# State rows ahead of the second stage, block sums on VectorE, two xo buffers, last rows stored in parts

## The chip, the core and the metric

The kernel runs on one core of a Trainium2 chip. The metric is the device time of one execution in microseconds. A core has TensorE (PE: matmuls, with PEld for the weight loads), VectorE (DVE), ScalarE (ACT), GpSimd (POOL) and SyncE (SP, which here issues all DMAs). Each engine runs its own instructions in order and waits on semaphores for the others.

## The reference

Three steps, all in fp32:

```
x: (8, 8, 512, 64), state: (8, 8, 32, 64)          # batch, head, row, dim
a  = softmax(x @ state^T / 8);  xread = a @ state   # per batch and head
a2 = softmax(state @ x^T / 8);  sread = a2 @ x
X  = concat(xread, sread) per batch -> (8 * 544, 512)
h  = X @ w_in (512 x 1024); s = h * softmax(h)
ln = (s - mean) / sqrt(var + 1e-6) * g;  X2 = ln @ w_out (1024 x 512)
out = leaky(X2 @ w_in2 (512 x 2048)) @ w_out2 (2048 x 512)     # leaky(v) = max(0.01 v, v)
```

The weights come as 64-bit floats and are narrowed in the kernel. Each batch has 512 x rows and 32 state rows; the 8 x 32 state rows are gathered into one block of 256 rows, which the code calls batch 8 (`B`).

## The kernel before, in words

Every matrix is kept as a high and a low part (`hi`, `lo`), and each product is three matmuls (`mm3`, L98 to L103): hi times hi, hi times lo, lo times hi. A split is a cast on ACT and a subtraction on DVE (L105 to L107) or on POOL.

*First stage.* For each batch: attention, then h (`h1`, L391) for four blocks of 128 rows, softmax and layer norm on those rows (`solu_norm`, L363), transposes (`tr`, L419), and the second product by w_out (`x2`, L439) in four parts. Each part is copied by ACT into the buffer xo (L453) and stored by SP to a scratch tensor xs in DRAM (L454). For the state rows `h1s` (L405) forms the first product in four steps from srs, the split of the collected state rows (`split_srs`, L799), with w_in loaded again in four parts (`load_wi`, L183); its norm follows in the last step, and `x2` for batch 8 has two parts.

*Second stage* (`second`, L748). Batches go in four pairs, hidden columns in eight chunks of 256. For each pair and chunk, `h2` (L642) forms the four blocks of the hidden layer with seven block products in place of eight (sums and differences of blocks of the weights, S1 to S4, and of x, T1 to T4), accumulating in PSUM banks X, Z and Y, and `out2` (L674) multiplies by w_out2 and adds into oacc on DVE (L689), eight tiles per chunk, through four PSUM banks. For the first pair the chunk's weights are prepared as well: `split_chunk` (L516) narrows them on DVE (L152 to L159), forms the block sums on POOL (L528 to L532), splits them and stores them to scratch, from where later pairs load them. The state rows go through the second stage during the first pair: `h8` (L708) and `out8` (L725), whose x is loaded from xs by `load_x8` (L695) and split by `split_x8` (L700). In the kernel before `h8` and `out8` of a chunk run in the next chunk's iteration, and the second product of the state rows runs between the two halves of chunk 0. `first_x2` (L565) loads and splits x for the first pair, `load_x2`, `diff_x2` and `swap_x2` (L587 to L604) for the others; at a pair's last chunk `out2` stores each batch's 512 rows in one DMA (L692).

*The order.* The list PROGRAM (L839) emits the first stage: a letter names a function (dictionary `emit`, L805) and the digits its arguments; E is the second stage. The order of emission is a priority: the tile framework's planner orders each engine's instructions by it and by its own estimate of when each can start, allots buffers with the same tag (`bufs` of them) and sets all waits. Instructions of different steps can thus be interleaved on an engine; on the chip each engine keeps the planned order.

Of the kernel before, what the change touches and what calls it, by code (L numbers as in the profile page):

```python
# [20 lines left out]
P = 128  # L21
# [17 lines left out]
def attn_solu_leaky_kernel(  # L39
# [399 lines left out]
    def x2(b, u):  # L439
# [4 lines left out]
        for j in range(nd):  # L444
            d = slice((nd * u + j) * P, (nd * u + j + 1) * P)
            for f in range(NF):
# [4 lines left out]
                )  # L451
        o = slot("xo", [P, nd, nt], F32, f"xo{b}_{u}", bufs=1)
        nc.scalar.copy(o, pt.rearrange("p (j t) -> p j t", j=nd))  # L453
# [62 lines left out]
    def split_chunk(c, kind):  # L516
# [3 lines left out]
        if kind == 0:  # L520
# [6 lines left out]
            a11, a12, a21, a22 = v[:, 0, 0], v[:, 1, 0], v[:, 0, 1], v[:, 1, 1]  # L527
            tt = nc.gpsimd.tensor_tensor  # L528
            tt(s_[0], a21, a22, ALU.add)
# [35 lines left out]
    def first_x2(u):  # L565
# [5 lines left out]
        elif u == 1:  # L571
            tsub("T1", C[:, 1, 0], xin["B12"], xin["B11"])
            tsub("T3", C[:, 0, 1], xin["B22"], xin["B12"])
            split_x2("B11", xin["B11"])
            split_x2("T1", td["T1"])
            split_x2("T3", td["T3"])
        elif u == 2:
            tsub("T2", C[:, 1, 1], xin["B22"], td["T1"])
            tsub("T4", C[:, 0, 0], xin["B21"], td["T2"])
            split_x2("B21", xin["B21"])  # L580
            split_x2("B22", xin["B22"])
        else:
            split_x2("T2", td["T2"])
            split_x2("T4", td["T4"])
# [21 lines left out]
    def split_x2(n, src):  # L606
        t = xb(n)
        split(t[:, 0], t[:, 1], src)
# [32 lines left out]

    def h2(p, c, part, between=None):  # L642
        C = late("C")[:, c % 2]
# [5 lines left out]
        if part == 0:  # L649
            prod(X, p, c, "A11", "B11", True)  # L650
            nc.scalar.copy(C[:, 0, 0], X)  # L651
            prod(Z, p, c, "A12", "B21", True)
            tt(C[:, 0, 0], C[:, 0, 0], Z, ALU.add)  # L653
            prod(X, p, c, "S2", "T2", False)
            nc.scalar.copy(C[:, 1, 0], X)
            prod(Y, p, c, "S1", "T1", True)
            if between is not None:
                h8(between)
            prod(X, p, c, "S3", "T3", False)
# [14 lines left out]
    def out2(p, c, j, rs=(0, 1, 2, 3)):  # L674
# [3 lines left out]
        for r in rs:  # L678
# [9 lines left out]
            else:  # L688
                nc.vector.tensor_tensor(o[:, r, :], o[:, r, :], pt, ALU.add)  # L689
        if c == NC - 1 and rs[-1] == NR - 1:  # L690
            rows = out.rearrange("(b t) d -> b t d", t=ROWS)
            nc.sync.dma_start(rows[2 * p + j, :S, :].rearrange("(p r) d -> p r d", r=NR), o)  # L692

# [54 lines left out]
    def second():  # L748
# [4 lines left out]
        for i, (p, c) in enumerate(seq):  # L753
# [7 lines left out]
            if turn:  # L761
                load_x2(p + 1)
            if not i:
                h2(p, c, 0)
                x2(B, 0)
                h2(p, c, 1)
                x2(B, 1)
                load_x8()
                split_x8()
                split_chunk(1, 1)  # L770
                out2(p, c, 0)
                out2(p, c, 1)
                continue
            h2(p, c, 0, prev[1] if prev[0] == 0 else None)
            if turn:
                diff_x2(p + 1)
                swap_x2("B11", "B21")
            if i > 1:
                out2(*prev, 0)
# [3 lines left out]
            if turn:  # L783
                swap_x2("T1", "T3")
            if i > 1:
                out2(*prev, 1)
            if turn:
                swap_x2("T4", "B22")
            if prev[0] == 0:
                out8(prev[1])  # L790
            if new and new[0] == 0:
# [7 lines left out]
    def split_srs():  # L799
        t = slot("q6", [P, 2, NHP, B * NS], F32R, "srs")  # L800
        split(t[:, 0], t[:, 1], srT)
        return t[:, 0], t[:, 1]
# [49 lines left out]
    S7.1 X5.1 t6.0 h6.2 U7.0 h6.1 A7.0 X5.2 w4.1 X5.3 h6.3 t6.1 A7.1 U7.1 B7.0 B7.1 X5.0 h7.0  # L852
    t6.3 R7 D0 t6.2 X6.2 h7.1 X6.1 h7.2 t7.1 X6.3 t7.0 h7.3 c0.0 c0.1 s X6.0 D1 t7.2 w4.0 w4.2 G0 d0.0 G1 G2
    t7.3 D2 w4.3 G3 d0.1 X7.1 X7.0 D3 X7.3 t8.0 X7.2 t8.1 E
"""
# [30 lines left out]
```

## Time and profile before

| | |
|---|---|
| timed runs | 1225.47, 1223.44, 1223.0 us; median 1223.44 us |
| profiled execution | 1218.0 us |
| its span in the trace | 1216.2 us |
| TensorE busy | 1149.7 us (95%), 5416 matmuls |
| VectorE / ScalarE / GpSimd busy | 809.2 (67%) / 496.3 (41%) / 367.6 us (30%) |
| chain that ended last | PE 71%, DVE 12%, POOL 5%, issue 4%, ACT 4%, DMA 3% |
| granted clock, mean | 0.985 |

All times in the rows are from the start of the span. The profiled execution is shorter than the timed ones; sums are made against it. The page gives busy shares of the whole span, which has stages with different limits; the tables by stretch show one stage at a time.

### The profile page before, as it was taken

Reading aid. Unit: us, or ns where it says so; the run is one execution under the profiler, and the core shown is the slowest. Engines: PE = TensorE matmul, PEld = TensorE weight load, DVE = VectorE, ACT = ScalarE, POOL = GpSimd, SP = SyncE. Lnnn points to the kernel's source line nnn. Section 1 sums busy time; section 2 is a strip of 40 time slices with the busy share of each in tenths; the row PEclk is TensorE's granted clock in tenths of the full one; section 3 lists DMA queues with packets and bytes.
Section 4 is the critical chain, followed back from the end, with each engine's and each line's share of the span. In section 5 each row is a group of like instructions: output and inputs, shape, how many; then the busy total and the mean of one; then the engine's idle time right before and its main releaser. Section 6 shows DMA issues by size and latency. Waiting matters only on the chain.

```text
span 1216.2 us, 14127 instructions
## 1 busy us (share of the span) xinstructions
PE 1149.7 (95%) x5416; PEld 949.5 (78%) x5416; DVE 809.2 (67%) x1224; ACT 496.3 (41%) x783; POOL 367.6 (30%) x246
## 2 busy tenths in 40 slices
PE   4768999999999998989999999999999999999998
PEld 2647888878888887877777788888888888888886
DVE  6998777886787587568886872545864547634544
ACT  3565656565565445444333423222432224232221
POOL 2432202202112024566655421323222222223231
PEclk9879999999999999989999999999999999999999
DMA  9432332152062155454554375444564343635331
GB/s 305 166 94 37 120 107 55 63 148 70 24 185 78 44 190 207 180 202 176 209 212 153 150 259 207 158 153 149 203 241 169 134 178 125 255 120 193 112 131 70
DMA packets 65868, 183.38 MB, mean 151 GB/s; under 512 B 39560, under 2 KB 39560, under 8 KB 53512
## 3 DMA queue, kind: packets, MB, share of 16 engines
q1 hardware_dynamic: 65800, 182.47, 42.6%
q8 instruction: 43, 0.70, 0.2%
q14 instruction: 25, 0.20, 0.1%
HBM read 135.27 MB, written 47.19 MB: 150 GB/s over the span
## 4 chain that ended last, share of the span: by engine, by line
PE 71%; DVE 12%; POOL 5%; issue 4%; ACT 4%; DMA 3%; SPq 1%; POOLq 0%; ACTq 0%; DVEq 0%
PE o L101 8%; PE o L102 8%; PE o L103 8%; PE x L101 4%; PE x L103 4%; PE x L102 4%; PE hX L101 4%; PE hX L102 4%; PE hX L103 4%; PE h L101 2%; PE h L103 2%; PE h L102 2%; PE hY L103 2%; PE hY L101 2%; PE hY L102 2%
## 5 line engine op out<-in xcount | busy, mean ns | idle before, releaser
L689 DVE TENSOR_TENSOR oacc<-oacc,o 128x512 f32<-128x512 f32 x224 | 150.4, 684 | 66.1 <-PE o L103 66.0
L101 PE MATMUL x<-ln,w_out_hi 128*128 128x512 f32 (+1 forms) x288 | 110.6, 384 | 3.9 <-ACT xo L453 3.0
L103 PE MATMUL x<-ln,w_out_lo 128*128 128x512 f32 (+1 forms) x288 | 109.8, 381 | 0.0
L102 PE MATMUL x<-ln,w_out_hi 128*128 128x512 f32 (+1 forms) x288 | 109.3, 380 | 0.0
L667 POOL TENSOR_TENSOR gb<-C,gb 128x1024 fp32r<-128x1024 f32 x16 | 47.4, 2964 | 197.7 <-ACT gb L666 182.6
L667 POOL TENSOR_TENSOR gc<-C,gc 128x1024 fp32r<-128x1024 f32 x16 | 46.5, 2905 | 197.1 <-ACT gc L666 197.1
L101 PE MATMUL o<-misc,gc 128*128 128x512 f32 x256 | 99.8, 390 | 1.7 <-DVE oacc L689 1.7
L102 PE MATMUL o<-wo,gb 128*128 128x512 f32 x256 | 99.7, 390 | 0.0
L102 PE MATMUL o<-misc,gc 128*128 128x512 f32 x256 | 99.7, 390 | 0.0
L101 PE MATMUL o<-wo,gb 128*128 128x512 f32 x256 | 99.7, 390 | 0.0
L103 PE MATMUL o<-wo,gb 128*128 128x512 f32 x256 | 99.6, 389 | 0.0
L103 PE MATMUL o<-misc,gc 128*128 128x512 f32 x256 | 99.6, 389 | 0.0
L611 DVE SCALAR_TENSOR_TENSOR C<-C 128x512 f32<-128x512 f32 x64 | 78.0, 1219 | 1.5
L101 PE MATMUL hX<-xbT,w 128*128 128x512 f32 x192 | 75.9, 396 | 3.0 <-ACT C L651 3.0
L614 ACT ACTIVATE C<-hX 128x512 f32<-128x512 f32 x32 | 19.1, 598 | 142.8 <-PE hX L103 142.8
L102 PE MATMUL hX<-xbT,w 128*128 128x512 f32 x192 | 75.6, 394 | 0.0
L103 PE MATMUL hX<-xbT,w 128*128 128x512 f32 x192 | 75.6, 394 | 0.0
L101 PEld LDWEIGHTS x<-ln,w_out_hi 128*128 128x128 f32 x288 | 54.6, 190 | 15.0 <-ACT xo L453 3.3
L661 DVE TENSOR_TENSOR C<-C,hY 128x512 f32<-128x512 f32 x32 | 21.9, 685 | 65.2 <-ACT C L660 65.1
L653 DVE TENSOR_TENSOR C<-C,hZ 128x512 f32<-128x512 f32 x32 | 22.0, 686 | 64.6 <-PE hZ L103 63.1
L101 PE MATMUL h<-sw,a1T 128*128 128x512 f32 x128 | 54.9, 431 | 8.5 <-DVE e(0, 0)_491 L370 4.1
L102 PEld LDWEIGHTS x<-ln,w_out_hi 128*128 128x128 f32 x288 | 54.7, 190 | 10.3 <-DVE r L259 0.2
(736 smaller groups left out, 2956.0 us busy)
## 6 DMA issues: line engine op xcount, KB each, us to landing
w<-w2s SPq DMA_DIRECT2D x24, 2048.0 KB, 7.8
wi<-wsc SPq DMA_DIRECT2D x16, 1024.0 KB, 6.4
w2s<-w SPq DMA_DIRECT2D x8, 2048.0 KB, 7.6
wo<-wo2s SPq DMA_DIRECT2D x12, 1024.0 KB, 7.3
misc<-wo2s SPq DMA_DIRECT2D x12, 1024.0 KB, 6.2
xs<-xo SPq DMA_DIRECT2D x34, 256.0 KB, 2.4
xn<-in_x SPq DMA_DIRECT2D x32, 256.0 KB, 4.6
raw<-in_moe_w_in SPq DMA_DIRECT2D x8, 1024.0 KB, 5.3
```

The lines of the kernel that those rows point to most:

```text
L101: nc.tensor.matmul(o, ah, bh, start=start, stop=False, **kw)
L102: nc.tensor.matmul(o, ah, bl, start=False, stop=False, **kw)
L103: nc.tensor.matmul(o, al, bh, start=False, stop=stop, **kw)
L611: nc.vector.scalar_tensor_tensor(o, v, 0.01, v, ALU.mult, ALU.max)
L614: nc.scalar.activation(o, v, AF.Copy, scale=0.01)
L653: tt(C[:, 0, 0], C[:, 0, 0], Z, ALU.add)
L661: tt(C[:, 1, 1], C[:, 1, 1], Y, ALU.add)
L667: nc.gpsimd.tensor_tensor(g[:, 1, 0], C[:, 0], f32(g[:, 0, 0]), ALU.subtract)
L689: nc.vector.tensor_tensor(o[:, r, :], o[:, r, :], pt, ALU.add)
```

## The change

Six edits. The buffer xo gets a second copy. The four block sums of a chunk go from POOL to DVE. In `second`, the two parts of `x2` for the state rows, their load and their split come ahead of chunk 0; chunk 0's `out2` goes into chunk 1 as for all other chunks; `h8` of a chunk runs in that chunk (chunk 1 makes 0 and 1), behind the fourth product; `out8` of the chunk before runs behind the second product (in chunk 1 behind the last). The last chunk's rows are stored as each tile of 128 rows is done. srs moves from buffer q6 to q2, and the split of T1, which lies in q2, to the last step of `first_x2`. The end of PROGRAM is reordered: the state rows' first product ahead of chunk 0's weights and of the x splits; `w4.1`, already emitted two lines above, is emitted again.

```diff
-        o = slot("xo", [P, nd, nt], F32, f"xo{b}_{u}", bufs=1)
+        o = slot("xo", [P, nd, nt], F32, f"xo{b}_{u}", bufs=2)
@@ split_chunk
-            tt = nc.gpsimd.tensor_tensor
+            tt = nc.vector.tensor_tensor
@@ first_x2
             split_x2("B11", xin["B11"])
-            split_x2("T1", td["T1"])
             split_x2("T3", td["T3"])
...
         else:
+            split_x2("T1", td["T1"])
             split_x2("T2", td["T2"])
@@ h2
-    def h2(p, c, part, between=None):
+    def h2(p, c, part, first=(), then=()):
...
             tt(C[:, 0, 0], C[:, 0, 0], Z, ALU.add)
+            for f, v in first:
+                f(v)
             prod(X, p, c, "S2", "T2", False)
             nc.scalar.copy(C[:, 1, 0], X)
             prod(Y, p, c, "S1", "T1", True)
-            if between is not None:
-                h8(between)
+            for f, v in then:
+                f(v)
             prod(X, p, c, "S3", "T3", False)
@@ out2
-        if c == NC - 1 and rs[-1] == NR - 1:
-            rows = out.rearrange("(b t) d -> b t d", t=ROWS)
-            nc.sync.dma_start(rows[2 * p + j, :S, :].rearrange("(p r) d -> p r d", r=NR), o)
+            if c == NC - 1:
+                rows = out.rearrange("(b t) d -> b t d", t=ROWS)[2 * p + j, :S, :]
+                nc.sync.dma_start(rows.rearrange("(p r) d -> p r d", r=NR)[:, r], o[:, r, :])
@@ second
+            old = c - 1 if p == 0 else NC - 1 if (p, c) == (1, 0) else -1
+            first = [(out8, old)] if old >= 0 else []
+            then = [(h8, k) for k in ([0, 1] if c == 1 else [c])] if p == 0 and c else []
+            if (p, c) == (0, 1):
+                first = []
             if not i:
-                h2(p, c, 0)
                 x2(B, 0)
-                h2(p, c, 1)
                 x2(B, 1)
                 load_x8()
                 split_x8()
-                split_chunk(1, 1)
-                out2(p, c, 0)
-                out2(p, c, 1)
-                continue
-            h2(p, c, 0, prev[1] if prev[0] == 0 else None)
+            h2(p, c, 0, first, then)
...
-            if i > 1:
+            if i:
                 out2(*prev, 0)
...
             h2(p, c, 1)
...
+            if (p, c) == (0, 1):
+                out8(0)
-            if i > 1:
+            if i:
                 out2(*prev, 1)
...
-            if prev[0] == 0:
-                out8(prev[1])
@@ split_srs
-        t = slot("q6", [P, 2, NHP, B * NS], F32R, "srs")
+        t = slot("q2", [P, 2, NHP, B * NS], F32R, "srs")
@@ PROGRAM
-    t6.3 R7 D0 t6.2 X6.2 h7.1 X6.1 h7.2 t7.1 X6.3 t7.0 h7.3 c0.0 c0.1 s X6.0 D1 t7.2 w4.0 w4.2 G0 d0.0 G1 G2
-    t7.3 D2 w4.3 G3 d0.1 X7.1 X7.0 D3 X7.3 t8.0 X7.2 t8.1 E
+    t6.3 R7 s w4.0 w4.1 D0 t6.2 X6.2 h7.1 X6.1 h7.2 t7.1 X6.3 t7.0 h7.3 G0 G1 w4.2 w4.3 c0.0 c0.1 t7.2
+    X6.0 G2 G3 D1 t7.3 D2 d0.0 X7.1 t8.0 X7.0 t8.1 d0.1 X7.3 D3 X7.2 E
```

## Rows read from the trace of the kernel before

**Rows 1.** Busy time by stretch: start:end, length, then PE, PEld, DVE, ACT, POOL, PEclk, DMA

```profile
430.00:480.00 50.00, 45.38 (x207) 36.87 (x206) 39.20 (x53) 25.61 (x37) 17.93 (x13) 0.97 0.55 200
480.00:560.00 80.00, 74.21 (x379) 62.98 (x377) 55.60 (x54) 35.34 (x48) 49.57 (x28) 0.96 0.57 211
560.00:705.00 145.00, 136.25 (x648) 112.50 (x647) 115.15 (x129) 56.61 (x69) 83.81 (x45) 1.00 0.43 165
618.12:645.64 27.52, 26.36 (x127) 21.91 (x126) 22.47 (x26) 10.72 (x13) 17.89 (x11) 1.00 0.38 153
```

**Rows 2.** TensorE's waits, 430 to 705 us: total us, times, longest us

```profile
PE o L101 <- DVE oacc L689: 9.0, 8, 1.7
PE x L101 <- ACT xo L453: 3.0, 1, 3.0
PE hX L101 <- ACT C L651: 3.0, 1, 3.0
PE hZ L103 <- POOL w L523: 1.7, 1, 1.7
PE x L101 <- ACT ln L106: 0.8, 1, 0.8
PE tr L432 <- DVE e(8, 0)_3976 L388: 0.8, 1, 0.8
```

**Rows 3.** Timeline, 449 to 463 us: start, length, engine, line, operation, idle before

```profile
449.61 3.86 POOL L529 TENSOR_TENSOR ws<-wn 128x256 f32<-128x256 f32 x1 [12.67 <-DVE wn L159]
...
456.69 1.06 ACT L533 CAST w<-ws 128x1024 fp32r<-128x1024 f32 x1 [6.14 <-POOL ws L532]
...
458.60 1.11 ACT L368 ACTIVATE e(8, 0)_3976<-hs,nm(8, 0)_3974 128x1024 f32<-128x1024 f32 x1
...
462.40 0.32 SPq L535 DMA_DIRECT2D w2s<-w  x1
462.81 0.38 SPq L454 DMA_DIRECT2D xs<-xo  x1
```

**Rows 4.** Timeline, 469 to 473 us, around the wait for xo

```profile
469.77 0.59 ACT L453 COPY xo<-x 128x512 f32<-128x512 f32 x1 [1.98 <-DMA xs<-xo]
...
470.41 0.50 PE L101 MATMUL x<-ln,w_out_hi 128*128 128x512 f32 x1 [3.05 <-ACT xo L453]
...
472.31 0.63 PE L103 MATMUL x<-ln,w_out_lo 128*128 128x512 f32 x1
```

**Rows 5.** Timeline, 502 to 520 us: x of the state rows goes out and back

```profile
502.38 0.34 SPq L454 DMA_DIRECT2D xs<-xo  x1
...
506.22 0.37 SPq L696 DMA_DIRECT2D misc<-xs  x1
...
517.15 0.39 PE L102 MATMUL h<-misc,w 128*128 128x256 f32 x1 [0.73 <-DVE misc L703]
```

**Rows 6.** Timeline, 640 to 644 us: the leaky step beside POOL's subtraction

```profile
640.02 2.40 POOL L667 TENSOR_TENSOR gc<-C,gc 128x1024 fp32r<-128x1024 f32 x1 [5.24 <-ACT gc L666]
...
641.11 2.38 DVE L611 SCALAR_TENSOR_TENSOR C<-C 128x1024 f32<-128x1024 f32 x1
```

**Rows 7.** POOL's groups, 430 to 720 us: busy us, mean ns, idle before

```profile
L529 POOL TENSOR_TENSOR ws<-wn 128x256 f32<-128x256 f32 x8 | 13.7, 1715 | 20.6 <-DVE wn L159 20.6
...
L531 POOL TENSOR_TENSOR ws<-wn 128x256 f32<-128x256 f32 x8 | 6.3, 792 | 0.0
```

**Rows 8.** DVE's groups, 430 to 720 us: busy us, mean ns, idle before

```profile
L653 DVE TENSOR_TENSOR C<-C,hZ 128x512 f32<-128x512 f32 x9 | 6.2, 685 | 10.0 <-PE hZ L103 8.5 <-ACT C L651 1.4
...
L563 DVE TENSOR_TENSOR C<-xbB,C 128x1024 f32<-128x1024 f32 x2 | 2.4, 1221 | 0.0
```

**Rows 9.** DVE's timeline, 612 to 690 us: the first difference for the next pair

```profile
666.26 1.23 DVE L563 TENSOR_TENSOR T<-xin 128x1024 f32<-128x1024 f32 x1 [5.08 <-DMA xin<-xs]
```

**Rows 10.** DMA issues: operation, count, KB each, median us from issue to landing

```profile
xs<-xo SPq DMA_DIRECT2D x34, 256.0 KB, 2.4
```

**Rows 11.** Line 882, the end of the program: count, ns min/median/max, first and last start

```profile
L882 SPq EVENT_SEMAPHORE  x7: 17/28/3371, 1211.8 to 1216.2; - x7
```

## The prediction

> **What bounds the kernel now.** I read four views, in this order. First the page: TensorE is busy 95% of the span and leads the chain of waits with 71%, so the time is TensorE's matmuls, which this change does not touch in number, plus the stretches where TensorE stands idle or runs at a lower clock. So the question is only which idle TensorE time goes and which comes.
>
> Second, the table of busy time by stretch [rows 1]. Before 430 us nearly all idle time lies in the first 120 us, ahead of everything in the change. From 430 to 480 us TensorE is idle 50.0 - 45.4 = 4.6 us, from 480 to 560 us 80.0 - 74.2 = 5.8 us, from 560 to 705 us 145.0 - 136.3 = 8.7 us. From 705 us on the page's slices show it full up to the last stores. All that this change can give back therefore lies between 430 and 705 us, where the state rows pass from the first stage to the second and the first pair of batches runs through its eight chunks, and at the end.
>
> Third, the waits of TensorE from 430 to 705 us [rows 2]: 9.0 us in eight waits of the output products for VectorE (DVE) to add an earlier one, 3.0 us for the copy to xo, 3.0 us for the copy of X to C, 1.7 us for a weight low part from GpSimd (POOL), 0.8 us twice for the last row blocks of the first stage, and 0.7 us for the state rows' x [rows 5].
>
> Fourth, the timeline around each. *State rows.* POOL takes its block sums at 449.6 us; the first lasts 3.86 us. ScalarE (ACT) stands with the cast of the sums (L533) until 456.69 us, having waited 6.14 us, and behind it in ACT's order is the exp of the state rows, at 458.60 us [rows 3]. *xo.* SyncE (SP) issues the w2s store of the same chunk at 462.40 us, once POOL is done, and the store of xo, queued behind it, at 462.81 us [rows 3]; the single xo buffer is free again at 469.77 us, and TensorE goes on at 470.41 us after 3.05 us; a matmul then takes 0.63 us [rows 4] instead of the 0.38 us of the page's groups: the clock has fallen from its upper level (2.4 GHz) to the lower (1.2 GHz) for a while after the idle time, and the stretch has a granted clock of 0.97, the next one 0.96, against 1.00 from 560 us on [rows 1]. *x of the state rows.* Its last part is stored at 502.38 us, SP issues the load at 506.22 us, and the product can start at 517.15 us, 0.73 us late [rows 5].
>
> **The change part by part.**
>
> *1. Two xo buffers, and the sums off POOL, 430 to 480 us.* The copy no longer waits for the store in front of it; the sums no longer hold the cast, so the exp of the state rows comes about 5 us earlier, and in the new emission order the state rows' products and norms come ahead of the x splits and chunk 0. Of the 4.6 us I take 3.05 (xo) and 0.8 (e(8,0)) as gone; the 0.8 for the transposes of batch 7 stays, since its norm is not touched. With the xo wait goes the slow clock: 24 matmuls from 470.41 us took some 7.2 us to issue against 24 x 0.227 = 5.4 us at the pace that the output products keep (six in 1.36 us), 1.8 us. Together 5.6 us. Bounds: 0, if something else (the splits on DVE) is as late, and 6.4 us.
>
> *2. The second product of the state rows in front of chunk 0.* It moves 11.5 us of TensorE work (two times 48 half-width matmuls) forward; nothing is added. It frees the w_out buffers earlier, so the weights of chunk 1 are split sooner, and it covers the x splits. Its SP work moves too: two stores of xo and the load of x. Cost: chunk 1 now makes both h8(0) and h8(1), and out2 of chunk 0 is moved into chunk 1, so between the last x2 product and h8(0) only 7 + 4 products of 1.36 us remain, 15.0 us. In the kernel before the read-back of x took 17.2 us: some 2.4 us from the end of the product to the store at 502.38 us, and 14.8 us from there to 517.15 us [rows 5]. That adds a wait of 2.2 us; queued behind it on TensorE is everything. If SP is free sooner than at 506.22 us it vanishes, if the w2s store stands in front of it again it may be 4 us with a slow clock. I take 2.2 us and keep 0 to 4.
>
> *3. Order in the chunk.* h8(c) reads chunk c's weights in chunk c itself instead of in the next one, so the buffer for the chunk after next is free half an iteration sooner; the wait for POOL (1.7 us) goes with it. Two output products of the state rows leave the end of the iteration, where they were the ninth and tenth to ask for one of four banks, and come after two products of 1.36 us. In rows: the leaky of 128x1024 (L611) takes 2.38 us instead of 1.22 us because POOL runs L667 from 640.02 to 642.42 us [rows 6, 8], the adds behind it come late, and the tenth fill waits 1.2 us. With 2.7 us of products in between, a lag of 1.2 us is covered. From 480 to 560 us I take the 5.8 us of idle as gone, and 2.8 us of slow clock behind the 3.0 us wait (27 matmuls from 536.5 to 543.2 us took 6.7 us, at the usual pace 3.9 us); less the 2.2 us of step 2 and 0.8 us for a ragged start, 5.6 us. From 560 to 705 us four such waits of 1.2 us and one of 0.5 us, 5.3 us, go. The other two of 1.7 us each at 668 and 673 us have another cause: DVE stood 5.08 us at the first difference for the next pair, whose x had not landed [rows 9]. The loads still follow the last raw weights; I take one of the two as gone, 1.7 us.
>
> *4. Block sums on DVE.* Four of 128x256 for each of eight chunks. No such row on DVE exists; 128x1024 takes 1.22 and 128x512 0.69 us [rows 8], so 1.04 ns an element and 0.16 us fixed, 0.42 us each, 1.7 us a chunk (lower bound 1.3 us, when the fixed part overlaps; upper bound that one of the four is also held by POOL as L611 was, 1.2 us more). POOL loses the same sums, 1.7 us for the first of them and about 0.8 us for the second [rows 7]. Per iteration DVE has 22.5 of 27.5 us busy, TensorE 26.4 [rows 1]: with 1.7 more, 24.2 us, it stays under TensorE's 26.4 us, but its casual slack falls from 3.9 to 2.2 us. I charge 2.0 us in all (bounds 0 and what the rivals say).
>
> The Trainium skill's page "SBUF — State Buffer" (section "Who interferes with whom") speaks against this part: a DVE instruction with two SBUF inputs and a GpSimd instruction that reads SBUF exclude each other for a whole instruction. The trace agrees: L611, with two SBUF inputs, ends 1.07 us after L667, its own length after POOL's end. By that rule a sum can be held for all of POOL's 2.40 us, so the sum above would lose up to 2.4 us a chunk on DVE; this is the second rival.
>
> *5. Last rows stored in parts.* At the end SP waits 3.37 us for the last 1 MB store [rows 11]. A 256 KB store lands 2.4 us after issue [rows 10], of which 0.34 us is the issue [rows 5]: a wait of 2.05 us, 1.3 us less (bounds 0 and 3.4). The other three parts go out under the products. For earlier pairs six more issues on SP hide under TensorE.
>
> *6. Order of the program, srs in another buffer, one more load of w4.1.* srs no longer waits for the last h, but its product still needs that h's bank; T1 now waits for srs, hidden by the state rows' second product. The extra 1 MB load goes out in a stretch in which the page's DMA row shows one or two tenths. Zero, with 2 us to either side, as the planner orders all of it anew.
>
> **Sum.** 5.6 + 5.6 + 5.3 + 1.7 - 2.0 + 1.3 = 17.5 us. The profiled execution took 1218.0 us (1216.2 us of span): 1200.5 us. The three timed runs have a median of 1223.44 us, 5.4 us above the profiled one; the same gain gives 1205.9 us, and 1206 is my figure.
>
> **The rivals.**
>
> *A. New waits take half of it.* x of the state rows late by 4 us with a slow clock, and a wait of about 1 us in each of five iterations because DVE has little slack. For it: rows 1 and 9, DVE busy and in order. Against: the banks' waits had one cause, and ten fills in a row are gone. Gain 17.5 - 9.5 = 8 us: 1215.5 us.
>
> *B. DVE becomes the bound: slower.* The place is chunks 1 to 6. The sums cost 1.7 us and are held for 2.4 us: 22.5 + 4.1 = 26.6 us busy, and DVE's own waits, 5.0 us an iteration now, have to shrink to zero to stay near TensorE's 26.4 us. If three of them stay, an iteration takes 29.6 us, 2.1 us more than now; six of these are 12.6 us, and the 5.3 and 1.7 us of step 3 do not come; steps 1, 3 (first part) and 5 give back 5.6 + 2.8 + 1.3 us at most. Time 1223.4 + 12.6 - 9.7 = 1226.3 us. It decides from 29.1 us an iteration on. Against it: POOL loses its sums, so the casts for which DVE waits come earlier.
>
> *C. The change does not arrive.* The order of instructions is a planner's, by its own times; it may put the state rows and the sums where they stood, with other waits of the same size. Only xo and the tail remain, less the 2 us of the sums: 3.05 - 2 + 1.3 = 2.3 us, within 0.2%: 1221.1 us.
>
> *D. All waits go,* the clock stays up and DVE keeps pace: 4.6 + 1.8 + 5.8 + 2.8 + 8.7 + 1.3 = 25 us: 1198.5 us.
>
> **How the numbers follow.** Forecast 0.55 (its own range 1200 to 1212 us), A 0.22, B 0.10, C 0.06, D 0.07. About 2.4 us (0.2%) is what a measurement of this kernel can tell from no change. Faster: forecast, A and D, 0.84; same: C, 0.06; slower: B, 0.10. The range runs from D's end to beyond A, 1199 to 1219 us; it leaves out B, C and the last of D.
>
> **What would show it.** Right: no wait of TensorE for xo; the exp of row block (8,0) within 2 us of its maximum; no block sums on POOL and DVE sums of about 0.4 us; iterations of the first pair at 26.4 to 27 us instead of 27.5; at most 2 to 3 us of wait at the first h8; a last wait of SP near 2 us. Wrong: waits of TensorE for oacc of 1 us or more in each chunk, sums on DVE of 1 us or more, or TensorE idle between the last x product of batch 7 and chunk 0.

## The result, and the profile after

The changed kernel is slower: 1234.88 us (median of four runs, 1232.46 to 1235.31) against 1223.22 us for the kernel before beside it, a ratio of 1.0102 [1.0076, 1.0128]. The forecast was 1206 us; the sign is wrong too. With four runs of each kernel the ratio may lean towards one of the two courses that a run can take before the change begins, of which the next paragraph tells.

The profiled execution took 1235.08 us, its span 1232.9 us, 16.7 us more than before. Some 6 us of that are not the change's. TensorE's first 1952 matmuls stand in the same order in both kernels. The 1789th begins R7 (the attention product `sr` of batch 7), yet it starts at 398.58 us in the one and at 404.51 us in the other. Across all profiles it starts either at 397.7 to 399.7 us or at 402.6 to 405.3 us, for kernels with and without the change, so I compare profiles from that product on: 817.6 us before, 828.4 us after, 10.8 us more. The ratio says 12.5 us (0.0102 x 1223).

Where the 10.8 us lie, with the start of a chunk taken at its first product `hX<-xbB` (matmuls that the change moves from one stretch to another are taken out: 11.5 us for the state rows' second product and 2.9 us for one h8): from R7 to chunk 0 +0.4 us; chunks 0 to 2 +1.9; chunks 3 to 7, 139.8 us before and 145.7 us now, +5.8; the rest, with a tail 1.5 us shorter, +2.7.

The table by stretch of the kernel after (columns as in [rows 1]; the fourth row is one iteration, the last two are 4 us each, behind a wait of TensorE):

```profile
430.00:480.00 50.00, 46.31 (x209) 37.39 (x209) 37.79 (x57) 24.75 (x37) 10.54 (x10) 0.93 0.36 127
480.00:560.00 80.00, 71.39 (x374) 60.45 (x373) 65.59 (x62) 36.14 (x50) 36.13 (x16) 0.96 0.67 247
560.00:705.00 145.00, 134.77 (x629) 111.33 (x627) 115.93 (x137) 50.83 (x63) 67.77 (x28) 0.98 0.46 172
605.09:633.85 28.76, 26.62 (x128) 21.87 (x126) 24.75 (x30) 10.53 (x13) 13.43 (x7) 1.00 0.48 183
456.00:460.00 4.00, 3.02 (x7) 2.22 (x8) 4.00 (x9) 2.74 (x4) 0.28 (x1) 0.56 0.00 0
594.00:598.00 4.00, 2.79 (x9) 2.28 (x10) 2.83 (x6) 1.70 (x3) 1.29 (x1) 0.81 0.58 218
```

Idle TensorE time is 3.7, 8.6 and 10.2 us in the three stretches; it was 4.6, 5.8 and 8.7 us. POOL is far less busy (10.5 instead of 17.9 us in the first, 67.8 instead of 83.8 us in the third), as meant, and TensorE gained nothing from it. The lower clock level was to go with the waits; it came back behind the new ones (0.56 and 0.81 in the last two rows). An estimate of its price: the share of the clock that was not granted, times the length, makes 3.5 + 3.2 + 2.9 = 9.6 us in the three stretches, against 1.5 + 3.2 + 0 = 4.7 us in [rows 1].

TensorE's waits of the kernel after from 430 to 705 us (columns as in [rows 2]):

```profile
PE hX L101 <- ACT C L662: 6.0, 3, 2.0
PE hY L101 <- DVE C L663: 4.5, 2, 2.4
PE h L102 <- DVE misc L705: 3.1, 1, 3.1
PE o L101 <- ACT oacc L742: 2.6, 1, 2.6
PE hX L101 <- ACT C L651: 2.0, 2, 1.3
PE x L101 <- ACT ln L106: 1.8, 1, 1.8
PE x L102 <- DVE ln L107: 1.0, 1, 1.0
PE tr L432 <- DVE e(8, 1)_3955 L388: 0.8, 1, 0.8
PE hX L101 <- DVE C L615: 0.5, 1, 0.5
```

Set beside [rows 2], nearly every name is new. The waits for xo (3.0 us) and for POOL's weight part (1.7 us) are gone, and so are the eight for oacc on L689 (9.0 us). In their place stand three of 2.0 us for the copy of X into C (L662), two for the sum of Y into C (L663), one of 3.1 us for x of the state rows (L705), one for the first tile of the state rows' oacc (L742), and two for the last norm of batch 7 (L106, L107). The total is 22.3 us, where [rows 2] and the 0.7 us for the state rows' x [rows 5] make 19.0 us. So the waits grew by 3.3 us and the clock took about 4.9 us more; together that is the 8.1 us from R7 to the end of chunk 7.

The costliest group, the waits for L662, is shown once in its place. Timeline of the kernel after, the iteration of 605 to 634 us (columns as in [rows 3], the bracket being the engine's idle time ahead of the instruction and what ended it):

```profile
602.38 3.41 POOL L523 TENSOR_TENSOR w<-wn,w 128x1024 fp32r<-128x1024 f32 x1
605.73 2.42 POOL L534 TENSOR_TENSOR w<-ws,w 128x1024 fp32r<-128x1024 f32 x1
605.82 1.15 ACT L151 ACTIVATE wn<-raw 128x1024 f32<-128x1024 f32 x1 [1.22 <-POOL w L523]
608.10 2.87 POOL L674 TENSOR_TENSOR gc<-C,gc 128x1024 fp32r<-128x1024 f32 x1
608.19 1.17 ACT L151 ACTIVATE wn<-raw 128x1024 f32<-128x1024 f32 x1 [1.22 <-POOL w L534]
610.93 2.84 POOL L539 TENSOR_TENSOR wo<-wn,wo 128x1024 fp32r<-128x1024 f32 x1
...
611.44 2.88 DVE L152 TENSOR_SCALAR wn<-wn 128x1024 f32<-128x1024 f32 x1
616.75 0.60 ACT L614 ACTIVATE c<-h 128x512 f32<-128x512 f32 x1 [3.64 <-PE h L103]
...
622.21 0.42 DVE L529 TENSOR_TENSOR ws<-wn 128x256 f32<-128x256 f32 x1
623.34 0.43 DVE L532 TENSOR_TENSOR ws<-wn,ws 128x256 f32<-128x256 f32 x1
623.69 0.68 DVE L615 TENSOR_TENSOR c<-h,c 128x512 f32<-128x512 f32 x1
624.40 0.62 ACT L724 CAST g<-c 128x512 fp32r<-128x512 f32 x1 [7.05 <-DVE c L615]
624.93 0.58 ACT L662 COPY C<-hX 128x512 f32<-128x512 f32 x1
625.56 0.50 PE L101 MATMUL hX<-xbT,w 128*128 128x512 f32 x1 [2.00 <-ACT C L662]
```

Read it from below. TensorE waits 2.00 us for X's bank, which L662 empties. ACT could have done that copy earlier, but the cast L724 stands ahead of it in ACT's order, and that cast waits 7.05 us for the leaky step of h8 on DVE (L615), whose input lay ready at 617.35 us (616.75 + 0.60). DVE comes to it 6.3 us later, because two whole narrowings (their first steps, L151, lie 2.4 us apart; before, two such steps lay 6.7 us apart in one iteration) and the four block sums stand in front, and because POOL works without a break from 600.0 to 613.8 us: L152 takes 2.88 us beside it, against 0.68 to 0.70 us wherever it runs without POOL, in all kernels here. Three engines' orders, none of them full, make one wait.

### The profile page after: what moved, and what is told of

Same layout as the page of the kernel before. It is cut to its first block, busy times and chain, and to the rows that moved or that the text cites. A ratio compares the mean times of both kernels' runs of the same rounds, so it can differ in the third digit from the quotient of the medians.

```text
span 1232.9 us, 14169 instructions
## 1 busy us (share of the span) xinstructions
PE 1158.6 (94%) x5416; PEld 955.0 (77%) x5416; DVE 835.4 (68%) x1256; ACT 494.4 (40%) x783; POOL 335.2 (27%) x214
## 4 chain that ended last, share of the span: by engine, by line
PE 69%; DVE 16%; issue 5%; ACT 4%; POOL 3%; DMA 2%; SPq 1%; POOLq 0%; DVEq 0%; ACTq 0%
PE o L101 7%; PE o L102 7%; PE o L103 7%; PE x L102 5%; PE x L101 5%; PE x L103 5%; PE hX L101 3%; PE hX L102 3%; PE hX L103 3%; PE h L101 2%; PE h L102 2%; PE h L103 2%; PE sr L305 2%; PE tr L432 2%; PE hY L101 2%
## 5 line engine op out<-in xcount | busy, mean ns | idle before, releaser
L611 DVE SCALAR_TENSOR_TENSOR C<-C 128x512 f32<-128x512 f32 x64 | 78.6, 1228 | 1.7
L663 DVE TENSOR_TENSOR C<-C,hY 128x512 f32<-128x512 f32 x32 | 21.9, 686 | 71.8 <-ACT C L662 71.7
L101 PEld LDWEIGHTS x<-ln,w_out_hi 128*128 128x128 f32 x288 | 54.9, 190 | 12.5 <-ACT ln L106 2.4
L102 PEld LDWEIGHTS x<-ln,w_out_hi 128*128 128x128 f32 x288 | 54.9, 191 | 11.5 <-DVE ln L107 1.3
L103 PEld LDWEIGHTS x<-ln,w_out_lo 128*128 128x128 f32 x288 | 54.9, 191 | 10.3
```

The costliest lines, as they stand in the source:

```text
L101: nc.tensor.matmul(o, ah, bh, start=start, stop=False, **kw)
L102: nc.tensor.matmul(o, ah, bl, start=False, stop=False, **kw)
L103: nc.tensor.matmul(o, al, bh, start=False, stop=stop, **kw)
L611: nc.vector.scalar_tensor_tensor(o, v, 0.01, v, ALU.mult, ALU.max)
L663: tt(C[:, 1, 1], C[:, 1, 1], Y, ALU.add)
```

## The experiments

Times are medians; ratios are to the kernel before, run beside each, in brackets the 95% interval. "In us" is a difference of ratios times 1223 us; the two intervals together leave it open by some 3 to 4.5 us. The traces give a second measure, one execution each, from R7 to the end: 817.6 us before and 828.4 us changed; e1 827.2, e2 819.3, e3 834.3, e4 820.6, e5 816.1, e6 830.7, e7 818.4, e8 815.7, e9 816.1, e10 830.3, e11 822.6, e12 816.3, e13 811.3, e14 806.7, e15 822.8, e16 817.1 and e17 816.7 us. Three questions in turn: which part of the change costs, what is behind the part that costs most, and what had caused the waits of the kernel before.

### Which part: one of them undone

**e1: the block sums back on POOL.**

```diff
-            tt = nc.vector.tensor_tensor
+            tt = nc.gpsimd.tensor_tensor
```

> The changed kernel (1234.9 us) with the four block sums of a chunk back on POOL, all else as changed. Theory Q (the order in the chunk: the two narrowings now run back to back on DVE ahead of the state rows' leaky step, the cast of g8 waits for that step at the head of ACT's queue, and the copy of X that frees a PSUM bank waits behind it): the sums are 1.5 us of the 8 us or so that stand in front of the leaky step, so the three waits of 2.0 us get shorter but the other idle time stays; 1228 to 1232 us. Theory S (the sums on DVE are the cost): back to 1223 us or less.

1230.4 us, 1.0075 [1.0052, 1.0097], 3.3 us back, which the noise does not tell from nothing; from R7 on the trace is 1.3 us shorter. The waits for L662 shrink from 2.0 to 0.3 us and chunks 3 to 5 take 27.7, 28.2 and 28.2 us (31.0, 28.8 and 29.9 us in the kernel after): with 1.7 us less ahead of L615, DVE's backlog clears that much sooner. Chunks 0 to 2 give half of that back (2.4 us longer, with waits of 3.3 us for L651 and for L705). So the sums have a part in the waits for L662; that they cost the kernel time is not shown, and the larger part of the loss remains.

**e2: the old loop of the second stage**, all else changed.

```diff
...
-            h2(p, c, 0, first, then)
...
+            h2(p, c, 0, prev[1] if prev[0] == 0 else None)
...
-            if (p, c) == (0, 1):
-                out8(0)
...
```

> The changed kernel with the second stage's loop as before (state rows' second product inside chunk 0, h8 and out8 one chunk later, out2 of chunk 0 in chunk 0); sums on DVE, two xo buffers, stores in parts and the new order of the first stage stay. Theory Q: the iterations of the first pair return from 29.1 us (mean of five) to about 28, the first three chunks lose their waits of 8.6 us; 1220 to 1225 us. Theory S: 1233 to 1236 us.

1225.66 us, 1.0022 [1.0004, 1.004]: the loop alone costs 9.8 us. The iterations are back at 27.54 us with the old wait of 1.18 us for oacc. What remains sits in the first stage; TensorE's waits there, kernel of e2, 430 to 705 us:

```profile
PE tr L432 <- DVE e(8, 1)_3955 L388: 2.2, 1, 2.2
PE x L101 <- ACT ln L106: 1.8, 1, 1.8
...
PE x L102 <- DVE ln L107: 0.9, 1, 0.9
...
PE tr L432 <- DVE e(8, 0)_3930 L388: 0.4, 1, 0.4
```

5.3 us in front of chunk 0. In the kernel after a low clock followed the same waits: 23 matmuls of the part of `x2` that waited took 8.2 us, where 24 take 5.7 us otherwise; in the trace of e2 the granted clock there is 1.00. The new order has used up the state rows' first products before the norm of batch 7's last block is ready; in the old one 24 of them lie behind that block's transposes and cover all but 0.8 us.

**e3: the old first-stage order**, with the new loop (PROGRAM, srs in q6, T1's split as before).

> The changed kernel with the end of the first stage ordered as before (PROGRAM's last lines, srs in q6, T1 split in the second step); loop, sums, xo and stores as changed. Theory Q: the first stage has no part in the loss, 1232 to 1237 us. Theory P (the new order of the state rows' first product costs: waits of 1.8, 1.0 and 0.8 us and a low clock at 455 to 475 us): 1225 to 1229 us.

1238.7 us, 1.0137 [1.0113, 1.0161]: 4.3 us worse still, at the edge of the noise, and 5.9 us by the traces. So the new loop needs the new first stage: in e3 the state rows' second product, ahead of chunk 0, stands 2.78 us for their norm (L107). The two parts don't add.

### The parts of the loop

**e4: h8 behind the fifth product and its copy**, so that L662 comes ahead of the cast.

```diff
             prod(Y, p, c, "S1", "T1", True)
-            for f, v in then:
-                f(v)
             prod(X, p, c, "S3", "T3", False)
             nc.scalar.copy(C[:, 1, 1], X)
             tt(C[:, 1, 1], C[:, 1, 1], Y, ALU.add)
+            for f, v in then:
+                f(v)
```

> The changed kernel with h8 emitted behind the product S3 T3 and its copy instead of in front of it, so that on ACT the copy of X (L660 here) stands ahead of the cast of g8; all instructions are the same. Theory Q: the waits of the hX products for the copy (6.0 us in three) and the low clock behind them go, iterations of 27 to 28 us, 1224 to 1229 us. Theories S and P: 1233 to 1236 us, since DVE's work and the first stage are untouched.

1227.02 us, 1.0031 [1.001, 1.0051], 8.7 us back (7.8 us by the traces). Iterations take 27.1 to 28.5 us. Its waits of TensorE, 430 to 705 us, begin with:

```profile
PE hX L101 <- ACT C L651: 6.1, 4, 2.1
PE o L101 <- ACT oacc L742: 3.1, 1, 3.1
```

L662 is no longer among them. But the narrowings still lie side by side, and their two first steps and a cast of theirs stand right ahead of the next chunk's first copy on ACT (L651): up to 2.1 us.

**e10 and e11: the state rows' second product back between the halves of chunk 0**, alone and with e4's edit.

```diff
+                h2(p, c, 0)
                 x2(B, 0)
+                h2(p, c, 1)
                 x2(B, 1)
                 load_x8()
                 split_x8()
+                split_chunk(1, 1)
+                continue
```

> The changed kernel with the state rows' second product between the two halves of chunk 0 again, all else as changed. If moving it forward is the main cost in the changed kernel too (alone it cost 11 us, e6 against e5): 1223 to 1226 us. If the changed first stage, with the norms ahead of the x splits, has paid for most of it: the stretch from the product R7 to chunk 3 gets 1 to 4 us shorter, 1231 to 1234 us.

> e4 (h8 behind the copy of X) and e10 together, on the changed kernel. Theory Q with both costs additive: 8 us from e4 and what e10 gives, 1219 to 1226 us, ratio to before 0.998 to 1.003. If both work on the same waits: no better than e4, 1.003.

e10 1231.53 us, 1.0076 [1.0053, 1.0098]; e11 1226.76 us, 1.002 [1.0001, 1.0039]. Alone it gives 3.2 us by the ratio, while the trace from R7 on is 1.8 us longer; on top of e4 it gives 1.3 us. Neither is more than the measurement tells from nothing. With the new first stage, no cost of that product's place is seen.

**e12: e11 with the old first-stage order as well.**

> As e11, with the end of the first stage ordered as before. In e5 the stretch from R7 to chunk 0 took 76.6 us, with the new first stage in the old loop (e2) 81.6 us: if these 5 us carry over, 1214 to 1221 us, ratio to before 0.993 to 0.999, the fastest so far; if the late norms cost it again behind (as e3 against the changed kernel, plus 4 us): 1.003 or more.

1222.73 us, 0.9995 [0.9975, 1.0014]. With h8 late and the state product inside chunk 0 the old first stage is the better one by some 3 us (the intervals overlap; 6.4 us by the traces); what is left of the change then is worth nothing, though xo, the tail and the sums stay in it.

### From the other side: the kernel before, with one part added

**e5: the second xo buffer and the last rows in parts alone.** e6 to e9, e13 and e14 are built on it.

> The kernel before with two of the six edits alone: two xo buffers and the last rows stored in parts. Both theories of the prediction's first and last term: the wait for xo (3.0 us) and the low clock behind it (1.8 us) go, the last store is 1.3 us shorter; 5 to 6 us under the kernel before, ratio 0.995 to 0.996. If the planner's new order gives the gain back elsewhere: ratio 0.999 to 1.002.

1220.61 us, 0.9972 [0.9951, 0.9992]: 3.4 us faster. From R7 to chunk 0 it takes 76.6 us instead of 79.8 us, since the wait of 3.05 us for xo and the slow clock behind it are gone and a wait of 1.5 us for the state rows' exp is new; most of that is given back in chunks 0 to 2 (87.3 us instead of 84.6 us), where new waits of 1.39 us (L651) and 0.83 us (L661) stand.

**e6: the state rows' second product ahead of chunk 0.**

> As e5, and the state rows' second product ahead of chunk 0 (out2 of chunk 0 stays in chunk 0, h8 and out8 one chunk later as before). The prediction's step 2: no cost beyond 0 to 4 us, since 7 + 8 + 4 products stand between it and the first h8; ratio to e5 0.998 to 1.002. If this edit is what costs the changed kernel its first chunks (waits of 8.6 us there): ratio to e5 1.004 to 1.007.

1230.49 us, 1.0063 [1.0038, 1.0087]: 11.1 us more than e5. Waits of the kernel of e6, 430 to 705 us:

```profile
PE o L103 <- POOL gb L667: 4.0, 1, 4.0
PE x L102 <- DVE ln L107: 4.0, 1, 4.0
PE hY L101 <- DVE C L661: 3.3, 2, 2.4
```

The moved product itself waits 4.0 us for the norm of the state rows. Behind it DVE is 2.4 us late with Y's sum and POOL 4.0 us late with its part of g, where in the kernel before nothing in chunk 0 waited. My sum had priced x's read-back alone.

**e7: h8 in its own chunk.**

```diff
-            if between is not None:
-                h8(between)
+            for k in between:
+                h8(k)
...
-            h2(p, c, 0, prev[1] if prev[0] == 0 else None)
+            h2(p, c, 0, ([0, 1] if c == 1 else [c]) if p == 0 else ())
```

> As e5, and h8 in its own chunk (chunk 1 makes two), out8 at the end of the next one as before. With one g8 buffer the cast of g8 can then only stand behind the copy of X on ACT. Theory Q1 (the two narrowings back to back on DVE cost by themselves): iterations of 28.5 us or more, ratio to e5 1.004 or more. Theory Q2 (they cost only because the copy of X waits behind the cast of g8): iterations of at most 27.6 us, ratio to e5 0.997 to 1.001.

1225.68 us, 1.002 [1.0001, 1.0038]: 5.9 us more than e5, 2.3 us by the traces. Chunk 2 takes 34.5 us (34.0 us in e5), with one wait of 6.3 us for a copy on ACT (L655), chunk 3 29.8 us (27.6 us) with 3.4 us (L651), and the later iterations 27.6 us, where 1.3 us for L651 has taken the place of 1.2 us for oacc. The ratio is that of Q1, the iterations are those of Q2, so this run does not decide between them. What the trace does show is that with h8 moved alone the two first steps of the narrowings lie 2.3 to 2.4 us apart from chunk 4 on (6.7 us in e5), that ACT's copies of the next chunk stand behind them, and that TensorE waits for those copies.

**e8: out8 ahead of out2's second half.**

> As e5, and out8 of the chunk before ahead of the second half of out2 instead of behind it, so that ten bank fills in a row become four, two and four with the products of h2's second half in between. The prediction's step 3 without h8 moved: the waits of 1.2 us in four iterations and of 0.5 us go, iterations of 26.4 us; 4 to 6 us under e5, ratio to the kernel before 0.990 to 0.993. If the wait only moves to another fill: ratio to e5 0.999 to 1.002.

1220.59 us, 0.9971 [0.9951, 0.9991], the same as e5. Iterations stay at 27.55 us, and the wait of 1.2 us now stands ahead of the last tile of out2, for an add of out8 (seven such waits for L742, 7.5 us in all). From the timeline of the kernel of e8:

```profile
618.77 2.41 DVE L611 SCALAR_TENSOR_TENSOR C<-C 128x1024 f32<-128x1024 f32 x1
621.10 0.67 DVE L742 TENSOR_TENSOR oacc<-oacc,o 128x512 f32<-128x512 f32 x1
621.83 0.50 PE L101 MATMUL o<-misc,gc 128*128 128x512 f32 x1 [1.16 <-DVE oacc L742]
```

The add that empties the bank comes behind the leaky step of 2.41 us, as in the kernel before. The row of fills was not taken apart, though: in both kernels TensorE fills four banks, makes two products and fills six banks in a row, and the edit swaps two groups of those six. So it was not that the state rows' fills came last: whoever comes last of the six waits. A kernel with the row broken and nothing else changed was not run.

**e9: the block sums on DVE.**

> As e5 (two xo buffers, last rows in parts; ratio to before 0.997), and the block sums on DVE. Theory Q: in the old loop order DVE has room for 1.5 us a chunk, the iterations stay at 27.5 us; ratio to e5 0.998 to 1.002. Theory S (the sums themselves cost 2 us a chunk or more): ratio to e5 1.006 or more.

1220.41 us, 0.9973 [0.9955, 0.9991]: nothing, with iterations of 27.53 to 27.57 us. The sums are dearer than 0.42 us here. Two of the four in the kernel of e9, 430 to 720 us:

```profile
L531 DVE TENSOR_TENSOR ws<-wn 128x256 f32<-128x256 f32 x8 | 14.3, 1794 | 0.0
L530 DVE TENSOR_TENSOR ws<-ws,wn 128x256 f32<-128x256 f32 x8 | 9.7, 1218 | 0.0
```

With 0.64 and 0.42 us for the other two that is 4.1 us a chunk. DVE's busy time from 560 to 705 us rises from 115.1 us in e5 to 135.2 us, and no time is lost: in this order DVE has room even for that.

### What made the waits: ACT's order and POOL's hold

**e13 and e14: e5 with POOL's subtraction at the first half of g on DVE**, e14 with the block sums on DVE too.

```diff
-            nc.gpsimd.tensor_tensor(g[:, 1, 0], C[:, 0], f32(g[:, 0, 0]), ALU.subtract)
+            nc.vector.tensor_tensor(g[:, 1, 0], C[:, 0], f32(g[:, 0, 0]), ALU.subtract)
```

> As e5, and the subtraction of g's first half (L667) on DVE instead of POOL, for all pairs, so that POOL no longer runs beside the leaky step of 128x1024 (L611). If POOL's hold of DVE is what makes the adds late by 1.2 us in each iteration of the first pair: L611 takes 1.2 us instead of 2.4, the waits for oacc fall under 0.3 us, iterations of 26.4 to 26.8 us, 4 to 5 us under e5. If DVE's own work in a row is what makes them late: the 1.2 us that L667 adds on DVE replace those of the hold, iterations stay at 27.5 us, ratio to e5 0.999 to 1.002.

> As e13, and the block sums on DVE (e9). POOL then keeps five subtractions an iteration; the two narrowings are held less often. If the hold is the cause of the waits: 1 us an iteration under e9, ratio to before 0.992 to 0.995, the fastest so far. If DVE's own work is: 27.5 us or more an iteration, ratio to e9 1.000 to 1.003.

e13 1213.97 us, 0.9925 [0.9897, 0.9952]; e14 1210.17 us, 0.9895 [0.987, 0.9919], the fastest of all, ahead of both kernels. DVE's groups of the kernel of e5 from 430 to 720 us (columns as in [rows 8]):

```profile
L159 DVE SCALAR_TENSOR_TENSOR wn<-raw,wn 128x1024 uint32<-128x1024 uint32 x16 | 30.2, 1887 | 0.3
...
L611 DVE SCALAR_TENSOR_TENSOR C<-C 128x1024 f32<-128x1024 f32 x8 | 18.9, 2358 | 0.0
```

and of the kernel of e14:

```profile
L159 DVE SCALAR_TENSOR_TENSOR wn<-raw,wn 128x1024 uint32<-128x1024 uint32 x16 | 21.7, 1356 | 0.2
...
L611 DVE SCALAR_TENSOR_TENSOR C<-C 128x1024 f32<-128x1024 f32 x9 | 10.9, 1215 | 0.1
...
L532 DVE TENSOR_TENSOR ws<-wn,ws 128x256 f32<-128x256 f32 x8 | 9.7, 1218 | 0.0
L529 DVE TENSOR_TENSOR ws<-wn 128x256 f32<-128x256 f32 x8 | 9.4, 1176 | 0.2
```

The leaky step falls from 2.36 to 1.22 us, and the narrowing's last step from 1.89 to 1.36 us. Two of the four sums now take 1.2 us instead of 0.42 us, as POOL runs beside them, and it does no harm where they lie. The stretch of 560 to 705 us in e14:

```profile
560.00:705.00 145.00, 143.95 (x698) 120.75 (x697) 124.73 (x154) 56.98 (x71) 52.88 (x24) 1.00 0.50 186
```

TensorE is idle 1.1 us of 145 (8.7 us in [rows 1]), iterations take 26.6 us, and DVE is busy 124.7 us, 9.6 us more than in [rows 1]. It is not DVE's busy time that bounds this stage. e13 alone keeps 1.05 us of the 1.2 us wait in chunks 3 to 5 and iterations of 27.4 us, against the 26.4 to 26.8 us expected; most of its gain lies in chunk 6 (30.5 us in e5, 26.9 us in e13). POOL's block sums have come to lie beside the leaky step, which is still held in part:

```profile
L611 DVE SCALAR_TENSOR_TENSOR C<-C 128x1024 f32<-128x1024 f32 x8 | 11.9, 1485 | 0.0
```

The sums have to leave POOL as well, which frees 18 us of POOL's time there (70.7 us in e13, 52.9 us in e14) and leaves 0.3 us of the wait.

**e15: the changed kernel with the cast of g8 on DVE**, so that nothing on ACT waits for L615; no product is moved.

```diff
-        nc.scalar.copy(g[:, 0], a)
+        nc.vector.tensor_copy(g[:, 0], a)
```

> The changed kernel with one instruction on another engine: the cast of the state rows' hidden block (g8, 128x512) goes from ACT to DVE, behind the leaky step on which it waits; no product is moved. Theory 1 (ACT's order makes the wait: the copy of X stands behind a cast that waits for DVE's backlog): the waits of 2.0 us of hX for the copy L662 go, iterations 605 to 720 us fall from 28.8 to 30.0 to some 27.5 to 28.4 us, and the time falls by 6 to 8 us, to 1227 to 1229 us, as when h8 was moved. Theory 2 (the two narrowings side by side and the earlier h8 product make it; the cast only stands in the same place): the time stays at 1233 to 1236 us and the wait takes another name.

1229.49 us, 1.0056 [1.0031, 1.0081], 5.6 us back, by the traces too; TensorE's waits of its kernel, 430 to 705 us, begin with

```profile
PE hX L101 <- ACT C L651: 6.0, 4, 1.9
PE hY L101 <- DVE C L663: 5.0, 4, 2.4
```

ACT's order made the wait for L662, as theory 1 says: it is gone, and chunks 3 to 7 take 140.7 us instead of 145.7 us. The gain is short of its 6 to 8 us, since 4.5 of the 6.0 us come back under the names L651 and L663 (theory 2 expected that of all of it); part of what stays is the clock, 0.98 and 0.99 in the second and third stretch instead of 0.96 and 0.98.

**e16: the changed kernel with POOL's subtraction at the first half of g on DVE; e17: with that and e15's edit.**

> The changed kernel with POOL's subtraction at the first half of g on DVE. Theory 1 (DVE is held by POOL's reads, and its backlog is what the changed order pays for): as in the kernel before (9 us there) the gain is 8 to 13 us, 1222 to 1227 us. Theory 2 (DVE is full by its own work in the changed order, so a further 1.2 us a chunk on DVE is paid): 1235 to 1240 us.

> The changed kernel with both: the cast of g8 and the subtraction of the first half of g on DVE. If the two causes are separate the gains add, 14 to 18 us: 1217 to 1221 us; if both act through the one backlog of DVE in front of the leaky step, the second adds no more than 2 us to the better of the two. Either way the state rows' product ahead of chunk 0 keeps it behind the 1210 us of the kernel before with the small edits, the sums and the subtraction on DVE.

e16 1219.99 us, 0.998 [0.996, 0.9999]: 14.9 us back (11.3 us by the traces), as much as the change had cost or more, with 1.2 us a chunk more work on DVE. e17 1221.64 us, 0.9996 [0.9977, 1.0014]: no better than e16. So the gains don't add; both act on one backlog. In e16 four waits for L662 are still there (6.0 us), but those for L651, L663, L705 and oacc have shrunk from 12.2 to 3.0 us, and chunks 1 and 2 take 56.9 us instead of 63.3 us. The comparison that tells more is e16 with e14: both have the second xo buffer, the stores in parts, the sums and the subtraction on DVE, and they differ in the order alone, the loop's and the first stage's. e16 is 10.4 us slower, by the ratios as by the traces. With the subtraction on POOL the same order costs 15.8 us (the changed kernel less e9; 12.3 us by the traces). So taking POOL away from the leaky step gives 9.5 us in the old order (e14 against e9) and 14.9 us in the new one, and most of what the new order costs stays.

## Why the prediction was wrong

By ratios the 12.5 us are: xo and tail -3.4 us (e5), the new first stage with the sums +6.1 us (e2 less e5; the sums by e9 nothing), the new loop +9.8 us (the change less e2). By the traces from R7 on the same three are -1.5, +3.2 and +9.1 us. The forecast had -17.5 us. Step by step:

1. *xo and sums off POOL, 5.6 us.* The xo wait is gone, and the exp of row block (8,0) starts at 454.30 us, 1.0 us after its maximum is done (452.13 + 1.22 us). But the order that brought this took the cover from batch 7's last block: 1.84 and 0.96 us of waits and the low clock of 456 to 464 us (0.56 and 0.58). "Its norm is not touched" was true and beside the point; what hid it was moved. Net +0.4 us.

2. *State product first, -2.2 us.* The wait for x came out at 3.1 us (0 to 4). The size of the rest was missed: the product's own input is late, and DVE and POOL are late behind it, 11 us in e6. The new first stage, which has the norms ready sooner, seems to take most of that away, as in the changed kernel little of it can be seen (e10, and e11 against e4).

3. *Order in the chunk, 5.6 + 5.3 + 1.7 us: the step that failed.* The waits that it named did go (9.0 us for oacc, 1.7 us for POOL's part), and others came: the loop costs 9.8 us (e2) where the step had 12.6 us of gain. "The buffer for the chunk after next is free half an iteration sooner" was right and was booked as a gain. It pulls both narrowings of the next chunk to the head of the iteration, on POOL, ACT and DVE at once, ahead of work for which TensorE waits (e7: +5.9 us by the ratio, +2.3 us by the traces). And the cast of g8 stands ahead of X's copy in ACT's order (e15: 5.6 us of the loss; with h8 moved, e4, 8.7 us). I had asked what a moved step frees and what it needs, and not what stands behind each of its instructions on ACT. And no new wait was given the low clock that the old ones had been given. Of the cause of the 1.2 us waits one half was misread: six fills stand in a row, not ten, and whether the row matters was not tested. The other half, POOL's hold of the leaky step, is shown by e14, which leaves 0.3 us of the wait with the row as it was; but L667 alone is not that hold, as e13 keeps 1.05 us.

4. *Sums on DVE, -2.0 us.* The 0.42 us is the price of a sum without POOL beside it. With the holds the four take 2.2 us a chunk in the kernel after and 4.1 us in e9, and in e9 that costs nothing. In the new order they stand in front of L615; what that costs is 3.3 us by the ratio and 1.3 us by the traces (e1), not clear of noise.

5. *Tail, 1.3 us.* Right. End of the program, kernel after (columns as in [rows 11]): 1.9 us instead of 3.4 us.

```profile
L884 SPq EVENT_SEMAPHORE  x7: 17/28/1915, 1230.0 to 1232.9; - x7
```

6. *Order, srs and the extra load, 0 within 2.* The order was worth 6.1 us the wrong way (3.2 us by the traces), by step 1's waits; srs and the load were not tried by themselves.

*The rivals.* B had the side, the place and the size: four of the five iterations from chunk 3 on lie at 28.8 to 31.0 us, where 29.1 us was to decide, and its 1226.3 us is the nearest of all. Its mechanism does not hold, so that this is in part luck. Its price of the sums, 1.7 + 2.4 = 4.1 us a chunk, is what e9 measures, and there it costs nothing: DVE's busy time is not the bound (24.75 of 28.76 us in the iteration shown, and e9 and e14 run with more). The hold by POOL makes DVE late in either order, but it is not what the new order costs: with L667 off POOL the waits for L662 still make 6.0 us (e16), and the order still costs 10.4 us (e16 against e14). What e4 and e15 show in its place is the price of one instruction standing behind another on ACT. A had its new waits, but expected about 1 us an iteration where 2.0 us came, and kept the rest of the gain. B had 0.10; held against 0.55 for a sum that took five separate waits as gone with their cause, that was too little.

The Trainium skill's page "SBUF — State Buffer" (section "Who interferes with whom") was the source of that rival. Its rule, that a DVE instruction with two SBUF inputs and a POOL instruction that reads SBUF contend, agrees with L611 (2.36 and 1.22 us) and with the held sums of e14. L152 is held too, with one input, 2.88 us beside POOL; for this the same section has a second rule, that DVE in a two-port mode contends with POOL. Without POOL L152 takes 0.68 to 0.70 us, where L156, with two inputs, takes 1.21 to 1.23 us; that L152 runs in such a mode would fit, but no row names its mode.

What stays open: how much of the 9.8 us of the loop each of its parts costs, as the parts do not add (e3, e4, e7, e12); why e17 is no faster than e16, though it has one wait less, and which rows of the first 120 us put R7 at 398 or at 404 us.

## What to carry to other kernels

When a step moves forward, list its instructions on every engine and ask what then stands behind each in that engine's order: here a 0.6 us cast on ACT, waiting 7 us for DVE, kept TensorE's bank. A buffer that comes free sooner is a trigger, not a gain: ask what it starts and beside what. And when a wait is put down to an instruction held by another engine, move that other engine's work first, before the order is touched, and look what takes its place: in e13 the moved subtraction made room for POOL's block sums beside the same step, and with both moved (e14) the kernel is the fastest here.

## What the runs showed of the hardware

The first stretch of these kernels took one of two courses: R7 starts at 397.7 to 399.7 us in 6 of the 19 profiles and at 402.6 to 405.3 us in 13. In the table by stretch, 60 to 120 us, of the kernel before (the first 60 us are alike):

```profile
60.00:120.00 60.00, 46.60 (x223) 36.85 (x223) 55.42 (x105) 36.08 (x65) 15.59 (x17) 0.88 0.29 70
```

and of the kernel after, with the same order of TensorE's instructions there:

```profile
60.00:120.00 60.00, 43.03 (x192) 34.80 (x191) 52.51 (x95) 34.29 (x62) 16.15 (x16) 0.77 0.26 65
```

The granted clock is 0.77 instead of 0.88, 31 matmuls fewer are done, and R7 starts 5.9 us later. Profiles of single executions can thus differ by 6 us ahead of any change; the timed ratios, over many runs, are what tells such a difference apart, and a trace is best compared from a common instruction on.

A wait of 2 us in the second stage was followed by the lower level of the clock, 1.2 GHz, or not: behind the 2.00 us wait at 595.2 us the granted clock is 0.81 and then 0.77 for 8 us, and the iteration takes 31.0 us; the one at 625.6 us has 1.00 throughout and 28.8 us. The first of these iterations has 0.6 us more of other waits, so an estimate of the clock's price is 1.6 us.
